# FFN, weight product and scores as 64x64 array tiles, two pairs of sums in turn

## The chip, the cores and the metric

The kernel runs on one core of a Trainium2 chip. The metric is the device time of one execution in microseconds. Where two kernels are compared, the ratio is the mean time of the one's fast runs over the mean of the other's from the same rounds on the same chip, so it is not quite the ratio of the medians quoted beside it. A ratio difference is turned into microseconds with 391 us for the kernel before.

The engines are TensorE (PE; its weight loads are PEld), VectorE (DVE), ScalarE (ACT), GpSimd (POOL) and SyncE (SP).

## The reference

Attention with RMS-normalised q and k (8 batches, 12 heads, 448 tokens, 64 per head), whose output, 3584 tokens by 768, goes through an FFN whose two up-projections are multiplied:

```python
q_n, k_n = rmsnorm(q, g_q), rmsnorm(k, g_k)
attn = softmax(q_n @ k_n.T / 8)
x = (attn @ v)                       # to (3584, 768)
out = (((x @ w1) * (x @ w2)) @ w3) @ w_out
```

The kernel computes `w3 @ w_out` once (the "weight product", w34) and works in bfloat16 with float32 sums.

## The kernel before

The program is a loop of 87 steps, called slots here. In each but the last three, TensorE computes two blocks of scores, ACT their exponentials; then comes (in most slots) a "v set", the product of probabilities with v or with ones; then fillers: FFN sums that keep TensorE busy; and last the "preps" of later heads: squares and alphas on ACT, reductions and scalings on DVE. Of PSUM the sums take eight banks: two score tiles of two banks each, and four banks for all other sums.

```python
sc_psum = ctx.enter_context(tc.tile_pool(name="sc_ps", bufs=2, space=PSUM))
mm_psum = ctx.enter_context(tc.tile_pool(name="mm_ps", bufs=4, space=PSUM))
# ...
def narrow(ps, n, lhsT, rhs, start, stop):          # one 128x128 block as four 128x32 tiles
    for h in range(4):
        nc.tensor.matmul(out=ps[32*h : 32*h+32, 0:n], lhsT=lhsT[:, 32*h : 32*h+32], rhs=rhs,
                         start=start, stop=stop, tile_position=(0, 32*h))

def ffn1_a(b, fi):                                   # x @ w1; ffn1_b (w2) likewise, evicted by DVE
    ps = mm_psum.tile([128, 512], FP, tag="mm", name="pa")
    for c in range(CM):
        narrow(ps, S, w1s[:, c, fi*128 : (fi+1)*128], xT[b][:, c, :], c == 0, c == CM - 1)
    a_sb = ffn_pool.tile([128, S], BF, tag="a_sb", name="a_sb")
    nc.scalar.copy(out=a_sb, in_=ps[:, 0:S])         # the ACT copy of the argument below
    # ...
# ...
for t in range(max(todo) + 1):
    # ... two qk_exp(n): scores on PE, exponential on ACT
    for i, kind in todo.get(t, []):
        pv_set(i, kind)
    # ... loads
    if t in W34_SLOTS: ...                           # weight product, slots 1 to 13
    elif not w34q:
        fill(int(old * room(t) / every + 0.5))       # so many fillers
    for n, part in mine: ...                         # preps
```

The softmax here doesn't subtract the row's maximum and nothing guards it: scores larger than these inputs give would overflow.

## Time and profile before

| | before |
|---|---|
| time, median of 2 runs | 390.64 us (388.81 to 392.47) |
| PE busy | 372.9 us, 96% |
| ACT busy | 265.5 us, 68% |
| DVE busy | 242.6 us, 62% |
| mean granted TensorE clock | 0.989 |

The last column of a group line is the idle time of its engine just before it and who ended it; for PE it is close to nothing. The prediction shows the lines. One more, from the list of waits (engine, line, whom it waited for, total us, times, longest us):

```profile
PE sc L297 <- ACT P L309: 1.3, 2, 0.8
```

PE practically never stands waiting for ACT to empty a score tile.

### The profile page before, as it was taken

To read this page: it belongs to the slowest core of one execution; us is meant where nothing else is said; L and a number is where in the kernel's file an instruction comes from. 1 tells how busy PE (TensorE), PEld (TensorE's weight loads), DVE (VectorE), ACT (ScalarE), POOL (GpSimd) and SP (SyncE) were. 2 spreads that over 40 slices of the span, in tenths; PEclk is the share of its full clock that TensorE was granted. 3 is DMA by queue.
4 is the path that set the end of the run, shared out by engine and by line. 5 is a ranking of instruction groups with operands and counts; after the bars stand their busy time and mean duration, and the time that the engine had idled before them with its cause. 6 is when DMAs were issued, how large, how long until landed. Compare 5 with 4: busy or idle time off the path is not lost.

```text
span 389.5 us, 17790 instructions
## 1 busy us (share of the span) xinstructions
PE 372.9 (96%) x8053; PEld 193.2 (50%) x8054; DVE 242.6 (62%) x398; ACT 265.5 (68%) x443; POOL 75.6 (19%) x131
## 2 busy tenths in 40 slices
PE   6979999999999997999989999999999999999995
PEld 2435555444544454454544554445544554556563
DVE  4789864557758774776568676667676685234232
ACT  3579896778688873888678956797788856730210
POOL 2525446322022202202202202201221000000000
PEclk9889999999999999999999999999999999999999
DMA  7999999769778939849969969958989565004005
GB/s 182 225 235 233 239 229 153 120 101 164 158 171 157 175 79 217 185 67 156 183 158 146 148 132 208 176 123 140 211 164 148 66 159 91 3 3 125 2 22 145
DMA packets 92975, 56.47 MB, mean 145 GB/s; under 512 B 56932, under 2 KB 86884, under 8 KB 92900
## 3 DMA queue, kind: packets, MB, share of 16 engines
q1 hardware_dynamic: 70208, 42.35, 51.7%
q0 software_dynamic: 21952, 12.33, 23.7%
q8 instruction: 63, 1.03, 1.1%
q10 hardware_dynamic: 740, 0.66, 0.7%
q14 instruction: 12, 0.10, 0.1%
HBM read 46.66 MB, written 11.01 MB: 148 GB/s over the span
## 4 chain that ended last, share of the span: by engine, by line
PE 78%; DMA 9%; DVE 4%; ACT 4%; SPq 3%; issue 2%; DVEq 0%; ACTq 0%
PE pa L354 17%; PE pb L354 17%; PE po L354 14%; PE pv L322 13%; PE sc L297 9%; PE wps L354 5%; DMA out_dram<-o_sb 5%; DMA k_sb<-in_k_dram 2%; SPq L129 2%; PE qkT_ps L272 2%; DVE ssq L214 2%; ACT P L309 1%; DVE o_sb L430 1%; DMA q_sb<-in_q_dram 1%; PE w3T_ps L367 1%
## 5 line engine op out<-in xcount | busy, mean ns | idle before, releaser
L309 ACT ACTIVATE P<-sc 128x896 bf16<-128x896 f32 x144 | 125.1, 913 | 29.4 <-PE sc L297 29.4
L354 PE MATMUL pa<-xT,w1s 128*32 128x448 bf16 x1536 | 83.9, 353 | 0.7 <-DVE xT L337 0.7
L354 PE MATMUL pb<-xT,w2s 128*32 128x448 bf16 x1536 | 83.8, 352 | 0.0
L152 POOL DMA_DIRECT2D v_sb<-in_v_dram x72 | 43.8, 620 | 200.5 <-PE pv L322 174.5
L354 PE MATMUL po<-w34s,abT 128*32 128x384 bf16 x1792 | 77.5, 326 | 2.8 <-DVE o_sb L430 2.8
L410 DVE TENSOR_TENSOR abT<-pb,a_sb 128x448 bf16<-128x448 f32 x64 | 39.9, 623 | 60.4 <-PE pb L354 46.5
L214 DVE TENSOR_REDUCE ssq<-sq 128x16 f32<-128x1024 f32 (+1 forms) x50 | 58.2, 1169 | 11.6 <-ACT sq L203 11.6
L397 ACT CAST a_sb<-pa 128x448 bf16<-128x448 f32 x64 | 33.9, 530 | 43.5 <-PE pa L354 43.5
L354 PEld LDWEIGHTS <-abT 128*32 128x32 bf16 x1792 | 48.1, 97 | 29.6 <-issue 3.3
L354 PEld LDWEIGHTS <-w1s 128*32 128x32 bf16 x1536 | 40.4, 97 | 34.3 <-issue 4.9
L354 PEld LDWEIGHTS <-w2s 128*32 128x32 bf16 x1536 | 41.4, 97 | 31.3
L430 DVE COPY o_sb<-po 128x384 f32<-128x384 f32 x56 | 30.5, 556 | 41.0 <-DMA out_dram<-o_sb 21.4
L297 PE MATMUL sc<-qkT 64*32 64x448 bf16 x1344 | 48.9, 357 | 1.8 <-ACT P L309 1.3
L236 DVE TENSOR_TENSOR qtmp<-q_sb,alpha 128x512 bf16<-128x512 f32 x48 | 32.9, 685 | 12.7 <-ACT alpha L225 12.4
L322 PE MATMUL pv<-P,v_sb 128*32 128x448 bf16 x576 | 36.0, 356 | 0.0
L337 DVE TENSOR_TENSOR xT<-pv,r 128x448 bf16<-128x448 f32 x48 | 29.6, 617 | 5.6 <-PE pv L322 3.7
L249 DVE TENSOR_TENSOR qks<-k_sb,alpha 128x512 bf16<-128x512 f32 x48 | 32.9, 685 | 0.0
L203 ACT ACTIVATE sq<-q_sb 128x512 f32<-128x512 f32 x48 | 30.2, 630 | 0.0
L203 ACT ACTIVATE sq<-k_sb 128x512 f32<-128x512 f32 x48 | 29.9, 622 | 0.0
L322 PEld LDWEIGHTS <-v_sb 128*32 128x32 bf16 x768 | 16.2, 95 | 24.2 <-issue 15.7
L297 PEld LDWEIGHTS <-qkT 64*32 64x32 bf16 x1344 | 12.3, 89 | 30.1 <-issue 28.8
L309 ACT ACTIVATE Pr<-sc 128x896 bf16<-128x896 f32 x24 | 22.0, 915 | 4.6 <-PE sc L297 4.6
(46 smaller groups left out, 247.2 us busy)
## 6 DMA issues: line engine op xcount, KB each, us to landing
out_dram<-o_sb SPq DMA_DIRECT2D x54, 192.0 KB, 3.5
q_sb<-in_q_dram SPq DMA_DIRECT2D x23, 256.0 KB, 3.9
k_sb<-in_k_dram SPq DMA_DIRECT2D x23, 256.0 KB, 4.9
q_sb<-in_q_dram SPq DMA_DIRECT2D x23, 192.0 KB, 4.4
k_sb<-in_k_dram SPq DMA_DIRECT2D x23, 192.0 KB, 5.2
v_sb<-in_v_dram POOLq DMA_DIRECT2D x24, 96.0 KB, 4.2
w3s<-in_moe_w_dram POOLq DMA_DIRECT2D x8, 256.0 KB, 9.7
w_outs<-in_moe_w_out_dram POOLq DMA_DIRECT2D x4, 384.0 KB, 11.9
```

Of the source, the lines that this page charges most:

```text
L152: nc.gpsimd.dma_start(out=dst.rearrange("p h j d -> p h (j d)"), in_=part.rearrange("p h j d -> p h (j d)"),)
L203: nc.scalar.activation(out=sq[:, t], in_=src[:, hs], func=AF.Square)
L214: nc.vector.tensor_reduce(out=s["ssq"][:, slice(*t), hs, :], in_=sq[:, slice(*t)], axis=AX, op=ADD)
L236: nc.vector.tensor_tensor(out=qtmp.transpose([0, 2, 1, 3]), in0=s["q"][:, hs], in1=alpha[:, 0, hs].unsqueeze(3).broadcast_to([NP, 2, J, D] ...
L249: nc.vector.tensor_tensor(out=qks[:, 1].transpose([0, 2, 1, 3]), in0=s["k"][:, hs], in1=alpha[:, 1, hs].unsqueeze(3).broadcast_to([NP, 2, ...
L297: nc.tensor.matmul(out=sc[c0 : c0 + 32, u, 0:S], lhsT=qkT[u * D : (u + 1) * D, pr, 1, k0 : k0 + 32], rhs=qkT[u * D : (u + 1) * D, pr, 0, 0:S],
L309: nc.scalar.activation(out=dst, in_=sc[:, :, 0:S], func=AF.Exp)
L322: nc.tensor.matmul(out=ps[h * HALF : (h + 1) * HALF, :], lhsT=w, rhs=s["P"][:, h, j, :] if j < NF else s["Pr"][:, h % 2, :], start=(j == 0 ...
L354: nc.tensor.matmul(out=ps[32 * h : 32 * h + 32, 0:n], lhsT=lhsT[:, 32 * h : 32 * h + 32], rhs=rhs, start=start, stop=stop, tile_position=( ...
L397: nc.scalar.copy(out=a_sb, in_=ps[:, 0:S])
L410: nc.vector.tensor_tensor(out=abT[bp][:, fi, odd * S : (odd + 1) * S], in0=ps[:, 0:S], in1=a_tiles.pop((b, fi)), op=MULT,)
L430: nc.vector.tensor_copy(out=o_sb[:, nh * NH : (nh + 1) * NH], in_=ps[:, 0:NH])
```

## The change

The intent: scores, FFN and weight product share one tile shape, 64x64, so that TensorE need not change shape between them. A 64x64 tile covers half the depth of a sum, and the two row halves of the array may not write one bank at the same time (point 3 of what the prediction takes from the Trainium skill). So two sums are worked on at once: in turn 0 the upper half adds to sum 0 and the lower to sum 1; in turn 1 they change over. Before it does, the matmuls of turn 0 must be through, which a nop on POOL's sequencer passes on. To hide that wait two pairs go in turn, so that a filler is now four sums in four banks. The weight product is moved into slots 8 to 11.

```diff
-    W34_SLOTS = {1: 2, 2: 1, 3: 2, 4: 3, 5: 1, 6: 1, 7: 3, 8: 1, 9: 1, 10: 2, ...}
+    W34_SLOTS = {1: 2, 2: 1, 3: 1, 4: 1, 5: 1, ...}
-        for c0 in range(0, NP, 32):
+        for c0 in range(0, NP, SC_W):               # SC_W = 64
-    def narrow(ps, n, lhsT, rhs, start, stop): ...
+    def swapped(pairs, n):
+        banks = [[mm_psum.tile([128, 512], FP, tag="mm", name="sw") for _ in range(2)] for _ in pairs]
+        turned = {}
+        for turn in range(2):
+            for p, pair in enumerate(pairs):
+                nk = pair[0][2]
+                for c in range(nk):
+                    for r in range(2):
+                        z = r ^ turn
+                        lhsT, rhs, _ = pair[z]
+                        for h in range(2):
+                            mm = nc.tensor.matmul(
+                                out=banks[p][z][64*h : 64*h+64, 0:n],
+                                lhsT=lhsT(c)[64*r : 64*r+64, 64*h : 64*h+64],
+                                rhs=rhs(c)[64*r : 64*r+64],
+                                start=(turn == 0 and c == 0), stop=(turn == 1 and c == nk - 1),
+                                tile_position=(64*r, 64*h), ...)
+                            if turn == 1 and (c, r, h) == (0, 0, 0):
+                                after(mm, turned[p])
+                if turn == 0:
+                    turned[p] = nc.gpsimd.nop()
+                    after(turned[p], mm)
+                if turn == 1:
+                    yield p, banks[p]
+    # w34_unit, ffn1, ffn2: two pairs each, evictions as before
-        for fi in range(CF):
-            fillers.append(ffn1_a); fillers.append(ffn1_b)        # shortened
+        for fi in range(0, CF, 2):
+            fillers.append(lambda b=b, fi=fi: ffn1(b, fi))
     # ... (the rest of the diff follows from this)
```

More of the change, by code (lines that the diff above doesn't have):

```diff
@@ L71 @@
     LAG = 8
+    SC_W = 64
     UNITS = 3.0
@@ L82 @@
     PREP = {'load': -7, 'sq0': -5, 'red0': -5, 'sq1': -4, 'red1': -4, 'alpha': -3, 'sc0': -3, 't0': -1, 'sc1': -2, 't1': -1}
-    W34_SLOTS = {1: 2, 2: 1, 3: 2, 4: 3, 5: 1, 6: 1, 7: 3, 8: 1, 9: 1, 10: 2, 11: 2, 12: 3, 13: 2}
+    W34_SLOTS = {1: 2, 2: 1, 3: 1, 4: 1, 5: 1, 6: 1, 7: 1, 8: 1, 9: 1, 10: 1, 11: 1, 12: 1, 13: 1}
     w1s = const.tile([128, CM, DFF], BF, name="w1s")
@@ L297, in qk_exp @@
                 nc.tensor.matmul(
-                    out=sc[c0 : c0 + 32, u, 0:S],
-                    lhsT=qkT[u * D : (u + 1) * D, pr, 1, k0 : k0 + 32],
+                    out=sc[c0 : c0 + SC_W, u, 0:S],
+                    lhsT=qkT[u * D : (u + 1) * D, pr, 1, k0 : k0 + SC_W],
                     rhs=qkT[u * D : (u + 1) * D, pr, 0, 0:S],
@@ L350, in w34_evac, with after @@
             nc.vector.tensor_copy(out=dst, in_=src)
-    def narrow(ps, n, lhsT, rhs, start, stop):
-        for h in range(4):
-            nc.tensor.matmul(
-                out=ps[32 * h : 32 * h + 32, 0:n],
-                lhsT=lhsT[:, 32 * h : 32 * h + 32],
-                rhs=rhs,
-                start=start,
-                stop=stop,
-                tile_position=(0, 32 * h),
-            )
+    def after(later, earlier):
+        tc.add_manual_dep(
+            later.ins,
+            earlier.ins.name,
+            mybir.DependencyInfo(
+                mybir.DependencyClass.Sync, mybir.DependencyReason.DATA
+            ),
+            reason="the other row half of the array takes over the bank",
+        )
+    def swapped(pairs, n):
+        banks = [
+            [mm_psum.tile([128, 512], FP, tag="mm", name="sw") for _ in range(2)]
+            for _ in pairs
+        ]
+        turned = {}
[8 more added lines that the diff above has]
+                            mm = nc.tensor.matmul(
+                                out=banks[p][z][64 * h : 64 * h + 64, 0:n],
+                                lhsT=lhsT(c)[64 * r : 64 * r + 64, 64 * h : 64 * h + 64],
+                                rhs=rhs(c)[64 * r : 64 * r + 64],
+                                start=(turn == 0 and c == 0),
+                                stop=(turn == 1 and c == nk - 1),
+                                tile_position=(64 * r, 64 * h),
+                                skip_group_check=True,
+                            )
+                            if turn == 1 and (c, r, h) == (0, 0, 0):
[5 more added lines that the diff above has]
+                    yield p, banks[p]
     def w3_transpose(fc):
@@ L370, in w3_transpose, with w34_unit, ffn1 @@
         w34_evac(w3T[:, :, fc * 128 : (fc + 1) * 128], ps, 0)
-    def w34_unit(fc, nh):
-        assert ("o", nh) in issued
-        ps = mm_psum.tile([128, 512], FP, tag="mm", name="wps")
-        for gc in range(CF):
-            lhsT = w3T[:, gc, fc * 128 : (fc + 1) * 128]
-            rhs = w_outs[:, gc, nh * NH : (nh + 1) * NH]
-            if W34_NARROW:
-                narrow(ps, NH, lhsT, rhs, gc == 0, gc == CF - 1)
-            else:
-                nc.tensor.matmul(
-                    out=ps[:, 0:NH], lhsT=lhsT, rhs=rhs,
-                    start=(gc == 0), stop=(gc == CF - 1),
-                )
-        w34_evac(w34s[:, fc, nh * NH : (nh + 1) * NH], ps[:, 0:NH], 1)
-    a_tiles = {}
-    def ffn1_a(b, fi):
-        ps = mm_psum.tile([128, 512], FP, tag="mm", name="pa")
-        for c in range(CM):
-            narrow(
-                ps, S, w1s[:, c, fi * 128 : (fi + 1) * 128], xT[b][:, c, :],
-                c == 0, c == CM - 1,
-            )
-        a_sb = ffn_pool.tile([128, S], BF, tag="a_sb", name="a_sb")
-        nc.scalar.copy(out=a_sb, in_=ps[:, 0:S])
-        a_tiles[b, fi] = a_sb
-    def ffn1_b(b, fi):
+    def w34_unit(fc):
+        pairs = [
+            [
+                (
+                    lambda gc, f=f: w3T[:, gc, f * 128 : (f + 1) * 128],
+                    lambda gc, nh=nh: w_outs[:, gc, nh * NH : (nh + 1) * NH],
+                    CF,
+                )
+                for nh in range(2)
+            ]
+            for f in (fc, fc + 1)
+        ]
+        for p, ps in swapped(pairs, NH):
+            for nh in range(2):
+                w34_evac(
+                    w34s[:, fc + p, nh * NH : (nh + 1) * NH], ps[nh][:, 0:NH], 1
+                )
+    def ffn1(b, f0):
         bp, odd = divmod(b, 2)
@@ L403, in ffn1_b @@
             abT[bp] = big_pool.tile([128, CF, TOK2], BF, tag="big", name="abT")
-        ps = mm_psum.tile([128, 512], FP, tag="mm", name="pb")
-        for c in range(CM):
-            narrow(
-                ps, S, w2s[:, c, fi * 128 : (fi + 1) * 128], xT[b][:, c, :],
-                c == 0, c == CM - 1,
-            )
-        nc.vector.tensor_tensor(
-            out=abT[bp][:, fi, odd * S : (odd + 1) * S],
-            in0=ps[:, 0:S],
-            in1=a_tiles.pop((b, fi)),
-            op=MULT,
-        )
@@ L417 @@
-    o_tiles = {}
-    def ffn2(bp, t, nh):
-        if nh == 0:
-            o_tiles[bp, t] = out_pool.tile([128, DM], FP, tag="o_sb", name="o_sb")
-        o_sb = o_tiles[bp, t]
-        ps = mm_psum.tile([128, 512], FP, tag="mm", name="po")
-        for fi in range(CF):
-            narrow(
-                ps, NH, abT[bp][:, fi, t * 128 : (t + 1) * 128],
-                w34s[:, fi, nh * NH : (nh + 1) * NH], fi == 0, fi == CF - 1,
-            )
-        last = (bp, t) == (B // 2 - 1, 6)
-        nc.vector.tensor_copy(out=o_sb[:, nh * NH : (nh + 1) * NH], in_=ps[:, 0:NH])
-        if nh == 0 and not last:
-            return
-        n0, n1 = (nh * NH, (nh + 1) * NH) if last else (0, DM)
-        for z, c0 in enumerate(range(t * 128, (t + 1) * 128, REST)):
-            bb, f = divmod(c0, S)
-            j, p = divmod(f, NP)
-            _, _, nj, t0, t1 = halves[p // REST]
-            r0 = (2 * bp + bb) * S
-            (nc.scalar if last and z else nc.sync).dma_start(
-                out=out[r0 + t0 : r0 + t1].rearrange("(p j) n -> j p n", j=nj)[
-                    j, :, n0:n1
-                ],
-                in_=o_sb[z * REST : (z + 1) * REST, n0:n1],
-            )
+        pairs = [
+            [
+                (
+                    lambda c, w=w, f=f: w[:, c, f * 128 : (f + 1) * 128],
+                    lambda c: xT[b][:, c, :],
+                    CM,
+                )
+                for w in (w1s, w2s)
+            ]
+            for f in (f0, f0 + 1)
+        ]
@@ new lines, in ffn1, with ffn2 @@
+        for p, ps in swapped(pairs, S):
+            a_sb = ffn_pool.tile([128, S], BF, tag="a_sb", name="a_sb")
+            nc.scalar.copy(out=a_sb, in_=ps[0][:, 0:S])
+            nc.vector.tensor_tensor(
+                out=abT[bp][:, f0 + p, odd * S : (odd + 1) * S],
+                in0=ps[1][:, 0:S],
+                in1=a_sb,
+                op=MULT,
+            )
+    def ffn2(todo):
+        pairs = [
+            [
+                (
+                    lambda fi, bp=bp, t=t: abT[bp][:, fi, t * 128 : (t + 1) * 128],
+                    lambda fi, nh=nh: w34s[:, fi, nh * NH : (nh + 1) * NH],
+                    CF,
+                )
+                for nh in range(2)
+            ]
+            for bp, t in todo
+        ]
+        for p, ps in swapped(pairs, NH):
+            bp, t = todo[p]
+            last = (bp, t) == (B // 2 - 1, 6)
+            o_sb = out_pool.tile([128, DM], FP, tag="o_sb", name="o_sb")
+            for nh in range(2):
+                nc.vector.tensor_copy(
+                    out=o_sb[:, nh * NH : (nh + 1) * NH], in_=ps[nh][:, 0:NH]
+                )
+                if nh == 0 and not last:
+                    continue
+                n0, n1 = (nh * NH, (nh + 1) * NH) if last else (0, DM)
+                for z, c0 in enumerate(range(t * 128, (t + 1) * 128, REST)):
+                    bb, f = divmod(c0, S)
+                    j, pp = divmod(f, NP)
+                    _, _, nj, t0, t1 = halves[pp // REST]
+                    r0 = (2 * bp + bb) * S
+                    (nc.scalar if last and z else nc.sync).dma_start(
+                        out=out[r0 + t0 : r0 + t1].rearrange("(p j) n -> j p n", j=nj)[
+                            j, :, n0:n1
+                        ],
+                        in_=o_sb[z * REST : (z + 1) * REST, n0:n1],
+                    )
@@ L447 @@
     fillers = []
+    rest = []
     def push_ffn(b):
         assert not wq
-        for fi in range(CF):
-            fillers.append(lambda b=b, fi=fi: ffn1_a(b, fi))
-            fillers.append(lambda b=b, fi=fi: ffn1_b(b, fi))
+        for fi in range(0, CF, 2):
+            fillers.append(lambda b=b, fi=fi: ffn1(b, fi))
         bp, odd = divmod(b, 2)
-        for t in range(3, 7) if odd else range(3):
-            for nh in range(2):
-                fillers.append(lambda bp=bp, t=t, nh=nh: ffn2(bp, t, nh))
+        rest.extend((bp, t) for t in (range(3, 7) if odd else range(3)))
+        while len(rest) > 1 or rest and b == B - 1:
+            two, rest[:] = rest[:2], rest[2:]
+            fillers.append(lambda two=two: ffn2(two))
@@ L527 @@
         w34q = [lambda: w3_transpose(0), lambda: w3_transpose(1)]
-        for fc in range(CF + LAG):
-            if fc < CF:
-                w34q.append(lambda fc=fc: w34_unit(fc, 0))
-            if fc + 2 < CF:
-                w34q.append(lambda fc=fc: w3_transpose(fc + 2))
-            if fc >= LAG:
-                w34q.append(lambda fc=fc: w34_unit(fc - LAG, 1))
+        for fc in range(2, CF):
+            w34q.append(lambda fc=fc: w3_transpose(fc))
+        for fc in range(0, CF, 2):
+            w34q.append(lambda fc=fc: w34_unit(fc))
         def prep_part(n, part):
```

## The prediction

> **What bounds the kernel now.** I read the page's busy shares first, then the chain of work that ended last, then the groups of instructions, then the timeline of one loop step ("slot": two score blocks with their two exponentials, one probability-times-v set, then FFN work as filler), and last the POOL timeline of the early stage.
>
> ```profile
> PE 372.9 (96%) x8053; PEld 193.2 (50%) x8054; DVE 242.6 (62%) x398; ACT 265.5 (68%) x443; POOL 75.6 (19%) x131
> ...
> PE 78%; DMA 9%; DVE 4%; ACT 4%; SPq 3%; issue 2%; DVEq 0%; ACTq 0%
> ...
> L309 ACT ACTIVATE P<-sc 128x896 bf16<-128x896 f32 x144 | 125.1, 913 | 29.4 <-PE sc L297 29.4
> L354 PE MATMUL pa<-xT,w1s 128*32 128x448 bf16 x1536 | 83.9, 353 | 0.7 <-DVE xT L337 0.7
> ...
> L354 PE MATMUL po<-w34s,abT 128*32 128x384 bf16 x1792 | 77.5, 326 | 2.8 <-DVE o_sb L430 2.8
> ...
> L397 ACT CAST a_sb<-pa 128x448 bf16<-128x448 f32 x64 | 33.9, 530 | 43.5 <-PE pa L354 43.5
> ```
>
> PE is 96% busy, carries 78% of the chain, and lost only 2.8 us to a late eviction (last column of the po row). ACT waits for PE (29.4 and 43.5 us), PE hardly ever for ACT. One slot in detail:
>
> ```profile
> 238.20 0.57 PE L297 MATMUL sc<-qkT 64*32 64x448 bf16 x16
> 238.70 0.75 PE L322 MATMUL pv<-P,ones 128*32 128x448 bf16 x12
> 239.28 0.36 PE L322 MATMUL pv<-Pr,ones 128*32 128x448 bf16 x4
> 239.47 1.31 PE L354 MATMUL pa<-xT,w1s 128*32 128x448 bf16 x24
> 240.60 1.31 PE L354 MATMUL pb<-xT,w2s 128*32 128x448 bf16 x24
> 241.84 0.57 PE L297 MATMUL sc<-qkT 64*32 64x448 bf16 x16
> ```
>
> Taken start to start: scores 0.50 us, v set 0.77, the FFN sums 1.13 and 1.24, together 3.64. Twenty-four 128x32 matmuls (six full 128x128 blocks) in 1.13 us are about 189 ns a block of 448 columns. What is not streaming is the change of tile shape: 0.11 us from FFN to scores (1.24 - 1.13), 0.13 from scores to v (0.50 - 2 x 0.187).
>
> ```profile
> 57.77 0.62 POOL L152 DMA_DIRECT2D v_sb<-in_v_dram  x1 [1.05 <-DVE qtmp L236]
> 58.89 0.59 POOL L152 DMA_DIRECT2D v_sb<-in_v_dram  x1 [0.50 <-DMA w2s<-in_moe_w_dram]
> 60.36 0.62 POOL L152 DMA_DIRECT2D v_sb<-in_v_dram  x1 [0.88 <-DMA w1s<-in_moe_w_dram]
> 61.76 0.60 POOL L156 DMA_DIRECT2D v_sb<-in_v_dram  x1 [0.78 <-DMA w2s<-in_moe_w_dram]
> ```
>
> These four are the last of POOL's initial loads. Each waits for an earlier transfer, so POOL's queue is clear of weights only at about 62 us; now nobody cares, because POOL has nothing else to do.
>
> **What the Trainium skill says.** (1) "TensorE: Matmul & The Clock Gate", section on why the gap is 56 ns: a warm matmul starts N / 2.4 GHz + about 2.5 ns after the last. For 448 columns that is 189.2 ns; the trace's 189 agrees. So the 128x32 form is already at the array's rate, and no other tiling of the full array has fewer columns to stream. (2) "TensorEngine Tiling (Array Packing)", Key Properties: a change of tiling mode drains TensorE. The 0.11 and 0.13 us agree. (3) The same page, Gotcha 1: different row tiles may not write one PSUM bank at once, and software must see to it. This is why the change needs two banks per pair and a wait at the changeover; no run yet shows it. (4) "PSUM — Partial Sum Buffer", Engine vs sequencer instructions: a nop is executed by the sequencer, which waits only for earlier instructions to be dispatched. Whether the changeover nop on POOL can therefore pass DMAs that still wait in POOL's queue, this trace cannot say.
>
> **The change, part by part.**
>
> *Streaming: 0 us.* A 128x128 block is four 64x64 matmuls instead of four 128x32 ones; FFN and weight product keep their counts, scores halve theirs (1344 to 672), but eight 64x32 tiles ran at once and now four 64x64 do: 448 columns either way.
>
> *Tile-shape changes: about -2.5 us.* FFN and scores now share a shape, but the v set between them stays 128x32. A slot with a v set still changes twice; only the 11 slots without one (from the tenth on) lose both changes: 11 x 0.24 = 2.6.
>
> *Granularity: the main cost.* A filler was one sum of 1.13 to 1.30 us, two or three a slot. It is now two pairs: 4 x 1.13 = 4.5 us (FFN1) or 4 x 1.30 = 5.2 (FFN2). The built instruction order shows that of slots 15 to 82, 38 get one unit and 30 get none. PE's mean work per slot is unchanged, but ACT works in program order, and PE's lead over it is two score buffers. Call a slot with a unit F, an empty one E, and let zero be the end of F's unit. In F, ACT does its two exponentials early, then must wait for the a_sb copies; the second comes only now: start 0.1, end 0.65 (530 ns). Then follow F's squares and alphas, which stand behind the copies: P us. Only then come E's exponentials, 0.913 each, done by 2.5 + P. PE meanwhile does E's scores and v set (0.50 + 0.86 with the change) and then stands before the next slot's second score block until 2.55 + P; with 0.19 + 0.1 + 0.86 after it, the next unit starts at 3.7 + P. If PE set the pace it would start at 2 x 1.36 = 2.7. Each F-E pair thus loses 1.0 + P. There are 19 FFN1 pairs of this kind; from the order, P is 1.25 (two squares) in six, 1.8 in three, 0.56 in two, 0 in eight: 14.0. Sum 19 x 1.0 + 14 = 33 us. For the 10 FFN2 units followed by an empty slot ACT has no copy to wait for, is idle at zero and finishes E's exponentials at 2.1: 0.65 us each, 6.5 in all. One double empty slot adds 1.
>
> *Banks: about +13.* A unit takes all four banks of the pool, where before a bank came round again after three other sums and sets (some 3.5 us). Now a v set's bank is wanted again 1.13 us after the set, by the unit's second pair, while VectorE needs 0.62 for it and may have a 1.2 us reduction ahead. Going through two stretches of the order by hand gave 0 to 0.6 us; I take 0.3 for 38 units and a little more where units follow each other.
>
> *Early stage: about +13.* The weight product (512 matmuls, 20 us) moves from slots 2 to 13 into slots 8 to 11, two halves at once. Slots 1 to 7 become ACT-bound (scores, squares) and end only about 3 us earlier; slots 8 to 11 cost 6.6 us each; slots 12 to 14 are empty and again at ACT's pace of about 3. Without more waits, slot 15 starts some 5 us later than the 73.9 of before. In addition the first changeover wants its nop at about 45, and POOL has all weight loads and a v load ahead of it in program order: 62 if it must be through with them, about 53 if the sequencer runs some DMAs ahead. I take a stall that makes the total +13 here (range 5 to 20).
>
> *Tail: +2.* The last units have nothing to overlap but each other; eviction of a pair by ACT then DVE (0.53 + 0.62) is just longer than the 1.13 of the other pair, and the final pair evicts two halves in a row.
>
> Sum: -2.5 + 33 + 6.5 + 1 + 13 + 13 + 2 = +66, so 456. The waits overlap in part (a late bank gives ACT time to catch up), so I take 450.
>
> **Rivals.** (a) The changeover is free and ACT's lag is absorbed: then only the shape changes remain and the time is about 388. For it: ACT is busy only 68%. Against it: ACT's order puts copies ahead of squares and exponentials, and two score buffers cannot bridge a 4.5 us unit. (b) Row halves with weights of 64 columns stream worse than quarters, or each changeover drains: 96 pairs of changeovers at 0.1 to 0.2 us would add 10 to 20 more, 465. Against it: the scores already use row halves at full rate. (c) POOL's nop is the main cost, at v loads in every stage: four descriptors of 0.62 us stand before a unit's nop in many slots. Against it: POOL reaches them a whole slot earlier. If wrong, 470 and more. (d) The early stage dominates and the steady one costs little: about 410.
>
> **Range and chances.** The steady loss could be half of what I sum (420), or banks and the nop could add 30 (480). Nothing supports a gain over 2%: the shape changes saved are 2.5 us of 390. Faster 0.03, within 2% 0.06, slower 0.91.
>
> **What would show it.** FFN groups of 24 matmuls still about 1.13 us (if longer, the streaming step is wrong). PE's wait for ACT before scores, 1.3 us now, should grow to some 30 to 50 us, and the granted clock stay high. PE's waits before FFN matmuls on DVE or ACT should show some 10 us, and one wait on POOL near 45 us of 5 to 17. Slot pairs should take about 9 us where two slots took 7.3. If slot pairs stay near 7.3, my account of ACT's order is wrong.

## The result, and the profile after

The changed kernel takes 472.01 us (median of 2 runs, 471.28 to 472.75) against 390.64. The ratio is 1.2075 (95% interval 1.193 to 1.222): slower by about 81 us, inside the stated range but above the stated 450.

From the page of the changed kernel: busy shares, granted clock in 40 slices, and the chain's shares.

```profile
PE 393.9 (84%) x7382; PEld 237.7 (50%) x7382; DVE 244.3 (52%) x398; ACT 265.5 (56%) x443; POOL 75.5 (16%) x131
...
PEclk9869679999998999999998999899999999999998
...
PE 53%; ACT 16%; DMA 12%; DVE 12%; issue 4%; POOL 1%; SPq 0%; DVEq 0%; ACTq 0%; POOLq 0%
...
L298 PE MATMUL sc<-qkT 64*64 64x448 bf16 x672 | 59.5, 366 | 30.8 <-ACT P L310 26.2
```

PE is now 84% busy, its share of the chain fell from 78 to 53%, and ACT (4 to 16%) and DVE (4 to 12%) took most of what it lost, although their own busy time has hardly changed. Work was not added; engines wait for each other. (PE's busy time did rise, from 372.9 to 393.9 us: a matmul before a wait is drawn longer than its turn, as told below, and more of them ran at half the clock.) The chain in order of time (start, length, what) shows one turn of it:

```profile
241.38 4.57 PE sw L379 x96
245.95 0.02 issue
245.97 0.53 ACT a_sb L440
246.51 0.23 ACT lnv L225
...
246.89 1.13 ACT sq L204 x2
248.03 1.62 ACT P L310 x2
249.65 0.04 issue
249.69 0.59 PE sc L298 x4
250.28 1.62 PE pv L323 x16
251.89 1.17 PE sw L379 x8
```

A unit ends at 245.95; only then does ACT copy the second sum, then alphas and squares, then two exponentials, and only at 249.69 may PE do the next slot's second score block. From unit to unit it is 251.89 - 241.38 = 10.5 us, the longest of the 19 FFN1 pairs of this kind in the trace; on average they take 9.5. The unit itself is not slow: 96 matmuls in 4.57 us are 1.14 per 24, as before. The waits of PE in the same trace:

```profile
PE sc L298 <- ACT P L310: 26.2, 45, 1.7
PE sw L379 <- POOLq L391: 14.5, 1, 14.5
PE sw L379 <- DVE xT L338: 9.6, 11, 1.3
PE sw L379 <- ACT r L333: 5.6, 6, 1.5
PE sc L298 <- ACT Pr L310: 3.0, 7, 0.4
```

The first and the last are waits for exponentials (29.2 us), the third and fourth for a v set's bank (15.2), the second the changeover nop. In the trace each v set that PE waits for on DVE stands directly behind a reduction or a scaling of the preps, and those on ACT behind two exponentials. The early stage, TensorE and below it POOL:

```profile
44.78 2.14 PE L379 MATMUL sw<-w_outs,w3T 64*64 64x384 bf16 x46 [0.90 <-DMA w_outs<-in_moe_w_out_dram]
61.44 4.58 PE L379 MATMUL sw<-w_outs,w3T 64*64 64x384 bf16 x64 [14.52 <-POOLq L391]
```

```profile
59.69 1.31 POOL L153 DMA_DIRECT2D v_sb<-in_v_dram  x2 [0.66 <-DMA w2s<-in_moe_w_dram]
61.39 0.60 POOL L157 DMA_DIRECT2D v_sb<-in_v_dram  x1 [0.38 <-DMA w2s<-in_moe_w_dram]
```

Turn 1 starts at 61.44, just after POOL's last queued load (61.39) has got past its own wait. The nop did not overtake DMAs that were still waiting.

Split by three marks, the first FFN matmul, the start of the last batch's FFN and the end of the span:

| stretch | before | after | difference |
|---|---|---|---|
| start to first FFN matmul | 71.5 | 96.0 | +24.5 |
| first FFN matmul to the last batch's FFN | 356.2 - 71.5 = 284.7 | 435.5 - 96.0 = 339.5 | +54.8 |
| rest | 33.3 | 35.5 | +2.2 |

An idle time in the profile starts at the modelled end of the last matmul. A block of four score matmuls that takes about 0.19 us start to start is drawn 0.38 long, so each wait contains about 0.19 us more than its idle figure. With that the steady stretch (the middle row) is nearly accounted for, as an estimate. Of the waits above, it holds 28.1 us for exponentials (49 times) and 14.5 for banks (16 times). So: exponentials 28.1 + 49 x 0.19 = 37, banks 14.5 + 16 x 0.19 = 18, one late transfer of q and k 1.7, three spells of 3.4 us at half the clock (from 147.0, 249.4 and 297.2 us) up to 5; less 6 for the six waits of the same stretch before, and less 2.5 for changes of shape saved (the prediction's figure, not measured). Together 53 of 54.8.

### The profile page after: what moved, and what is told of

Its sections match the earlier page's. It is cut to its first block, busy times and chain, and to the rows that moved or that the text cites. A ratio compares the mean times of both kernels' runs of the same rounds, so it can differ in the third digit from the quotient of the medians.

```text
span 471.0 us, 16496 instructions
## 1 busy us (share of the span) xinstructions
PE 393.9 (84%) x7382; PEld 237.7 (50%) x7382; DVE 244.3 (52%) x398; ACT 265.5 (56%) x443; POOL 75.5 (16%) x131
## 4 chain that ended last, share of the span: by engine, by line
PE 53%; ACT 16%; DMA 12%; DVE 12%; issue 4%; POOL 1%; SPq 0%; DVEq 0%; ACTq 0%; POOLq 0%
PE sw L379 47%; ACT P L310 8%; DMA w3s<-in_moe_w_dram 5%; DVE ssq L215 3%; PE pv L323 3%; ACT sq L204 3%; ACT a_sb L440 3%; DMA w2s<-in_moe_w_dram 2%; DMA v_sb<-in_v_dram 2%; DVE qtmp L237 2%; PE sc L298 2%; DVE xT L338 2%; DVE qks L250 2%; DMA qkT<-qks 1%; DVE o_sb L465 1%
## 5 line engine op out<-in xcount | busy, mean ns | idle before, releaser
L379 PE MATMUL sw<-xT,w2s 64*64 64x448 bf16 x1536 | 153.3, 354 | 9.9 <-ACT r L333 4.9
L379 PE MATMUL sw<-xT,w1s 64*64 64x448 bf16 x1536 | 159.9, 355 | 0.0
L379 PEld LDWEIGHTS <-w1s 64*64 64x64 bf16 x1536 | 91.5, 108 | 35.1 <-issue 11.9
L441 DVE TENSOR_TENSOR abT<-sw,a_sb 128x448 bf16<-128x448 f32 x64 | 40.0, 625 | 122.2 <-ACT a_sb L440 122.2
L379 PEld LDWEIGHTS <-w2s 64*64 64x64 bf16 x1536 | 87.6, 108 | 29.6 <-issue 17.1
L440 ACT CAST a_sb<-sw 128x448 bf16<-128x448 f32 x64 | 34.0, 532 | 106.2 <-PE sw L379 106.2
L298 PE MATMUL sc<-qkT 64*64 64x448 bf16 x672 | 59.5, 366 | 30.8 <-ACT P L310 26.2
L379 PE MATMUL sw<-w34s,abT 64*64 64x384 bf16 x1792 | 77.8, 323 | 5.2 <-DVE xT L338 5.0
L379 PEld LDWEIGHTS <-abT 64*64 64x64 bf16 x1792 | 57.9, 107 | 24.4 <-issue 10.7
L465 DVE COPY o_sb<-sw 128x384 f32<-128x384 f32 x56 | 28.6, 553 | 40.8 <-PE sw L379 40.8
L379 PE MATMUL sw<-w_outs,w3T 64*64 64x384 bf16 x512 | 24.2, 341 | 16.1 <-POOLq L391 14.5
```

What stands on the lines that cost most here:

```text
L298: nc.tensor.matmul(out=sc[c0 : c0 + SC_W, u, 0:S], lhsT=qkT[u * D : (u + 1) * D, pr, 1, k0 : k0 + SC_W], rhs=qkT[u * D : (u + 1) * D, pr, ...
L379: mm = nc.tensor.matmul(out=banks[p][z][64 * h : 64 * h + 64, 0:n], lhsT=lhsT(c)[64 * r : 64 * r + 64, 64 * h : 64 * h + 64], rhs=rhs(c)[6 ...
L440: nc.scalar.copy(out=a_sb, in_=ps[0][:, 0:S])
L441: nc.vector.tensor_tensor(out=abT[bp][:, f0 + p, odd * S : (odd + 1) * S], in0=ps[1][:, 0:S], in1=a_sb, op=MULT,)
```

## The experiments

The outputs are right. No run shows whether TensorE could wait for its own turn 0 without another engine.

| run | median us | ratio to before | 95% interval |
|---|---|---|---|
| the changed kernel | 472.0 | 1.2075 | 1.193 to 1.222 |
| e1_nop_on_sync | 499.1 | 1.2742 | 1.266 to 1.283 |
| e2_coarse_quarters | 409.7 | 1.0466 | 1.041 to 1.052 |
| e3_product_back | 447.0 | 1.1416 | 1.135 to 1.148 |
| e4_scores_64 | 390.0 | 0.9958 | 0.991 to 1.001 |
| e5_squares_before_copies | 419.7 | 1.0668 | 1.060 to 1.074 |
| e6_quarters_same_banks | 437.1 | 1.1122 | 1.107 to 1.118 |
| e8_one_pair | 423.3 | 1.0772 | 1.072 to 1.082 |
| e9_set_between | 410.6 | 1.0443 | 1.039 to 1.050 |
| e10_nop_split | 458.5 | 1.1751 | 1.171 to 1.180 |
| e11_before_sc64_preps_first | 388.1 | 0.9949 | 0.991 to 0.998 |
| e12_between_preps_first | 402.9 | 1.0350 | 1.029 to 1.041 |
| e13_both_repairs | 426.0 | 1.0929 | 1.088 to 1.098 |

**The nop on another sequencer.** On the changed kernel:

```diff
-                    turned[p] = nc.gpsimd.nop()
+                    turned[p] = nc.sync.nop()
```

> The changed kernel with one edit: the changeover nop goes to SyncE's sequencer instead of POOL's. Theory (the 14.5 us wait of PE near 45 us is POOL's queue of weight loads): that wait goes and the time falls by 12 to 17 us, to about 457. Rival (the nop stands behind PE's own matmuls, or the weights bind anyway): no change, 472. A third way: SyncE's queue holds loads and stores that wait too, and new PE waits on SyncE of over 5 us in all take the gain back.

The third way came true. The first FFN matmul starts at 80.7 instead of 96.0, so the early wait was POOL's queue. But SyncE's queue, with its loads and stores, made new waits all along the steady part (34.5 of the 37.9 us below after 94 us), and the whole became slower:

```profile
PEld L379 <- SPq L391: 37.9, 19, 3.5
PE sw L379 <- SPq L391: 30.5, 16, 3.1
```

**The same granularity with the old tiles.** On the kernel before: four sums to a filler, one after the other, each in its own bank.

```diff
-            fillers.append(lambda b=b, fi=fi: ffn1_a(b, fi))
-            fillers.append(lambda b=b, fi=fi: ffn1_b(b, fi))
+            fillers.append(lambda b=b, fi=fi: [(ffn1_a(b, f), ffn1_b(b, f)) for f in (fi, fi + 1)])
     # ... (four sums of ffn2 likewise)
```

> The kernel before, with its 128x32 tiles, its one-by-one banks and its early stage, but with fillers of four sums in one piece, as many and in the same slots as in the changed kernel. Theory (the steady loss is granularity against ACT's program order): 415 to 425. By the pair's reckoning the second copy now ends 0.5 us before the filler does, so an FFN1 pair loses the larger of 0.65 and about P - 0.1 (19 us in all), FFN2 pairs 6.5, a double empty slot 1, together 26, plus a few us of lower clock. Rival 1 (granularity is harmless, row halves and banks cost it all): below 398. Rival 2 (granularity is all of the steady loss): 445 to 450.

409.7, below the expected span: the pure size of the filler costs 0.0466 x 391 = 18 us. Its waits for exponentials are 14.5 us in 34 pieces, with 0.19 for each about 21:

```profile
PE sc L297 <- ACT P L309: 12.0, 28, 0.5
PE sc L297 <- ACT Pr L309: 2.5, 6, 0.4
```

There is no wait for a v set's bank. So neither rival holds: granularity is harmful, but it is a third of the steady loss, less than the theory had.

**The weight product as it was.** On the changed kernel: `w34_unit`, its order and W34_SLOTS from the kernel before.

> The changed kernel with the weight product put back as it was (128x32 tiles, one sum at a time, slots 1 to 13). Theory: the early stage loses its 20 us, so 450 to 454, and slot 15 starts near 74 us instead of 94. Rival (the early delay was hidden slack, ACT would have been waited for later anyway): 460 or more.

447, a little better than expected: 1.2075 - 1.1416 = 0.066, or 26 us, for the early stage. Its first FFN matmul starts at 71.5, 24.5 earlier; slot 15 starts at 69.6, not near 74, as slot 14 has no FFN sums here. None of the early loss was hidden slack. Its waits, with which the next versions are compared, are nearly those of the changed kernel without the early one:

```profile
PE sc L298 <- ACT P L310: 26.4, 45, 1.7
PE sw L390 <- DVE xT L338: 9.6, 11, 1.3
PE sw L390 <- ACT r L333: 4.9, 5, 1.5
PE sc L298 <- ACT Pr L310: 2.5, 6, 0.4
```

**Scores alone.** On the kernel before: score tiles 64 wide instead of 32.

> The kernel before with the scores alone in 64x64 tiles. Theory (streaming does not depend on the tile shape, a change of shape costs the same): 390, within 0.7%. Rival (64-column weights load or start more slowly): 168 score blocks at 0.05 us or more each, 399 and above.

0.9958, its interval just reaching 1: as expected, half the instructions and the same time.

**Preps ahead of the filler.** On e3, from slot 15 on:

```diff
+            for n, part in mine:
+                if part[0] != "t" and part not in ("load", "v"):
+                    prep_part(n, part)
             if t in W34_SLOTS: ...
             elif not w34q:
                 fill(...)
-            for n, part in mine: ...        # was here (shortened)
```

> The kernel with the product back (447 us), with the squares, alphas, reductions and scalings of a slot issued ahead of its filler, so that they stand before the copies in ACT's order. Theory (P sits between the late copy and the exponentials): PE's wait for the exponentials, 29 us there, falls by about 14 and the time to 430 to 436. Rival (the copy alone or VectorE sets the pace): under 4 us of change; or slower, if reductions and scalings that now stand before the products on VectorE hold up banks.

419.7: this order alone gives back 0.0748 x 391 = 29 us, twice what was expected, and the lines say why. PE's waits in this run:

```profile
PE sc L298 <- ACT P L310: 16.0, 46, 1.1
...
PE sc L298 <- ACT Pr L310: 2.6, 6, 0.4
```

Waits for exponentials fell from 28.9 us (26.4 and 2.5 in e3) to 18.6. The bank waits (9.6 and 4.9 in e3) are gone from the list altogether: DVE's reductions and scalings no longer stand between the unit's products and the eviction of the next v set, nor ACT's squares before its exponentials and evictions. With four banks held, the bank term was thus a matter of the order on DVE and ACT; but e2, with the old order and banks taken one by one, has none either, so it needs both. Exponentials 10.3, banks 14.5 and 16 waits fewer at 0.19 are 28 of the 29 us.

**Old tiles, the same banks and ends.** On e3, inside the unit:

```diff
-                for c in range(nk):
-                    for r in range(2): ...              # 64x64, row halves changing over
+                for c in range(turn * nk // 2, (turn + 1) * nk // 2):
+                    for z in range(2):
+                        lhsT, rhs, _ = pair[z]
+                        narrow(banks[p][z], n, lhsT(c), rhs(c), c == 0, c == nk - 1)
```

> The kernel with the product back, units of two pairs and four banks taken and finished at the same points, but each matmul a 128x32 quarter over the full depth: the two sums of a pair take half their depth in turn 0 and half in turn 1, so no row half and no changeover wait. Theory (row halves stream at full rate and the hidden changeover is free; what costs is that both sums end together and the banks): 443 to 451, as with row halves, PE's bank waits again about 14 us. Rival (row halves or the changeover themselves cost): about 410, as the coarse quarters with one sum after the other.

437.1, below the expected span, between the two and much nearer to row halves. Going from e2 to e6 (same tiles, but sums that end together and four banks held) costs 0.0656, 26 us; going from e6 to e3 (row halves and the changeover) 0.0294, 11 us. Its waits:

```profile
PE sc L298 <- ACT P L310: 21.6, 37, 1.4
PE sw L355 <- DVE xT L338: 9.0, 11, 1.3
PE sw L355 <- ACT r L333: 3.9, 3, 1.3
PE sc L298 <- ACT Pr L310: 2.5, 6, 0.4
```

The bank waits are back without any row half. Of the 11 us, exponentials and banks explain 28.9 - 24.1 = 4.8 and 14.5 - 12.9 = 1.6, and some ten fewer waits at 0.19 another 2; here the first sum of a pair ends one block earlier than the second, so its copy starts earlier. The traces of the two show two more differences in the steady part: e3 waits once for a late transfer of q and k (1.3 us), and it has one spell of 3.4 us at half the clock there (up to 1.7 lost), e6 none. That is about all of it, so nothing is left that would point to slower streaming in row halves.

**One pair to a filler.** On e3: units of one pair, two banks, nothing between its turns.

> The kernel with the product back, but with one pair to a filler (2 banks, 2.3 us) and so each changeover exposed: its second turn waits for its own first turn's last matmul and the nop. Theory (granularity and banks cost most of it, the changeover would cost little over its latency): bank waits near zero, about 0.3 to 0.5 us of PE idle at each of 92 changeovers, so 392 + 28 to 46 = 420 to 438. Rival (changeovers are cheap, 0.1 us): near 402. Rival (they are worse than the granularity): 450 or more.

423.3, as the theory expected. Waits for exponentials and v-set banks are not among its waits of PE; instead weight loads stand at every changeover:

```profile
PEld L390 <- POOLq L402: 49.1, 92, 0.8
```

Around one of them matmuls start at 231.94 and 232.42, 0.48 us apart where the rhythm is 0.19. That is 0.29 lost, times 92 about 27 us; the ratio says 30.

**The v set between the turns.** On e8: turn 0, v set, turn 1; in slots without a v set the scores stand between.

> As with one pair to a filler, but the v set (or, in slots without one, the scores) is issued between the two turns, so it hides the changeover; the last units go two pairs in turn. 64x64 row halves throughout FFN and scores. Theory (nothing is wrong with the row halves, only with when their sums end and what they hold): 390 to 402; some 15 second pairs of a slot keep an exposed changeover or a late bank. Rival (row halves cost by themselves): 420 or more.

410.6, missed: the changeover is hidden (its waits for POOL's nop are 5.1 us in 17 pieces instead of 49.1 in 92), which gained 13 us, but 17 remain against the kernel before. PE's list has 6.9 us for v-set banks, 4.5 for two late evictions before v sets and 3.8 for exponentials.

**The same, preps first.** e9 with the edit of e5.

> The v set between the two turns, and preps ahead of the filler. Without the second edit it stands 18 us above before. Theory (both sums still end together at the end of a slot, with the squares behind the copies): the order gives back a third to a half, 400 to 404. Rival (the 18 us are late banks of v sets between turns, which this does not touch): 408 to 412.

402.9, in time as expected; but by the ratios only 3.6 us came back, less than the expected third to a half of 18 and less than the medians suggest, because the kernel before was also quicker in that round. About 14 us remain. No group of waits before its matmuls is over 4 us; weight loads wait 6.2 us for the products on DVE and 5.6 for nops. I did not find one cause: it stays open.

**The nop split.** The changed kernel, SyncE's nop for the weight product only.

> The changed kernel with the changeover nop of the weight product alone on SyncE, that of the FFN on POOL as it was. Theory (of the early 20 us the wait behind POOL's weight loads is 15, the concentration into four slots 5; POOL costs nothing later): PE's 14.5 us wait gone, no SyncE waits after the early stage, the first FFN matmul near 81 us instead of 96, and 455 to 459. Rival (the time comes back later as other waits): 465 or more.

458.5 and 1.1751. The first FFN matmul comes at 81.9, 14.1 earlier than in the changed kernel, the 14.5 us wait is gone and no wait on SyncE or POOL is left. The rest of the list is nearly what it was (26.2, 9.6, 5.2, 3.0), so POOL's nop costs nothing here once its queue is clear. By this mark the early stage thus divides into 14 us of nop and 24.5 - 14.1 = 10 us of concentration.

**Both repairs.** e10 with the edit of e5.

> The changed kernel with both repairs: the weight product's nop on SyncE and the preps ahead of the filler. Theory (the two losses are independent): 472 - 15 - 27 = 430, 427 to 434. Rival (they overlap): 440 or more.

426.0, just under the expected span. From the ratios, 1.2075 - 0.0324 - 0.0748 would be 1.1003; it is 1.0929, 3 us less, which is within the intervals. The losses are independent as far as these runs can tell, and 36 us stay.

**A better version of the kernel before.** Scores 64 wide and preps first, on the kernel before.

> The kernel before with scores in 64x64 tiles and the squares, alphas, reductions and scalings ahead of the filler. PE waits only 1.3 us for exponentials there, so theory: 387 to 391, within 1% of before. Rival (the order has slack to give here too): 384 or less. Rival (products wait behind reductions on VectorE and hold banks): 394 or more.

388.1 and 0.9949, its interval below 1: faster than both kernels, though against the kernel before by half a per cent only. As e4 alone gave 0.9958, nothing shows that the order of the preps adds to it.

## Why the prediction was right

The direction and the range were right, and the mechanism is the one it named. By the ratios of e2, e6 and e3 the 81 us divide into 18 for the size of the filler, 26 for sums that end together in four banks held, 11 for row halves with their changeover, and 26 for the early stage. The early stage was sized too small, the sum was then discounted where nothing overlapped, and a loss of clock was left out. That the steady terms add up to 51 against 54.8 measured is partly luck: exponentials came out some 3 us below their term, banks some 5 above, and the clock's up to 5 us and the 6 us of waits that the kernel before had there were in no term.

- *Streaming costs nothing:* held. A unit runs at 1.14 us per 24 matmuls, and e4 and the balance of e6 and e3 agree.
- *The shape changes saved are small:* e4 and the steady sum fit it, but no run measured the 2.5 us by itself.
- *ACT's program order, 33 + 6.5 + 1 = 40.5 us:* held. The waits come to about 37 with their hidden part. The trace has the 19 FFN1 pairs that were counted. From a unit's end to the next unit's start they take 4.1 us on average (2.6 to 6.1), where 3.7 + P was reckoned, 4.4 on average, and 2.7 without a wait: some 27 us lost instead of 33. The FFN2 pairs lose the 0.65 each that was reckoned. Pairs take 9.5 us on average, banks included, where "about 9" was the sign named. In the pair shown above P is 1.5, not 1.8, and half the clock lengthens what follows, so that its 10.5 against the reckoned 4.57 + 3.7 + 1.8 = 10.1 proves less than it seems. e5, which takes P away, left 18.6 us of idle in 52 waits, about 28 with the hidden part, against 26.5 reckoned for the pairs without P.
- *Banks, 13:* about 18. The reason given, a reduction ahead of the eviction on DVE, is what the trace shows for two thirds of it and e5 removes; the other third is evictions on ACT behind exponentials.
- *Early stage, 13 (5 to 20):* this step failed in size. By the prediction's own mark, the start of slot 15, it is 94.0 - 73.9 = 20.1; e10 starts slot 15 at 79.9. So the concentration cost 6.0, where 5 was reckoned, and the nop 14.1, where 8 was: the 13 fits a nop at 53, that is a sequencer which runs ahead of its DMAs. It was 61.4, close to the 62 also named. By the first FFN matmul the loss is 24.5, because slot 14 had FFN sums before and has none now, and the time followed this mark (25 us between the changed kernel and e3). One reading was off: of the four POOL loads shown, said to wait for an earlier transfer each, the first is put down to a DVE instruction.
- *Tail, 2:* 2.2.
- *"The waits overlap in part, so I take 450":* this step failed. The undiscounted sum was 456, and with 24.5 for the early stage it would have been 467.
- *"The granted clock stay high":* failed in part. The mean fell from 0.989 to 0.96. The trace has half the clock from 20.7 to 30.9 us, where TensorE waits for preps and for the loads of w3, from 51.5 to 65.2, in the early stall and just after it, and in the three spells of the steady stretch. One of these follows the waits at 247 to 250 us: the next twelve v-set matmuls are drawn 1.31 us long instead of 0.75. From 94 to 435.5 the mean is still 0.99, so this was a few us and no more.

Of the rivals, (a) fell with the result; (b) was at most 11 us with the changeover, all but explained by ends, banks, a late transfer and the clock; (c) was right for the early stage and wrong for the rest (e10), so that its "470 and more" is near to 472 by chance; (d) fell, as the steady part is two thirds of the loss.

## What to carry to other kernels

When TensorE is full, a filler's size, the moment its sums end and what stands behind them in the other engines' program order are a cost of their own, even if no work is added; put work that others wait for ahead of copies that must wait for a long unit. A signal sent through another engine waited here for the transfers queued there before it (14.5 us on POOL, 30.5 in all on SyncE), so look at what is queued at that time, not at how busy the engine is. And two score buffers did not bridge a unit of 4.6 us.

## What the Trainium skill lacked or had wrong

- "PSUM — Partial Sum Buffer", Engine vs sequencer instructions, says that a nop waits only for the dispatch of earlier instructions. It doesn't say that software DMAs which wait for a semaphore count as not yet dispatched: here the nop's effect came at 61.44 us, after POOL's last waiting load had started at 61.39.
- "TensorEngine Tiling (Array Packing)", Key Properties and Gotcha 1, gives no price for a change of mode or for ordering two row halves on one bank. Here a change of mode cost 0.11 to 0.13 us, and an exposed changeover through another sequencer about 0.29 us (e8).
- "TensorE: Matmul & The Clock Gate", Part 1, has the cold state after at least one idle window of about 3.4 us, though its section on a second HAM failure mode tells of short idles between groups of matmuls that do it too. Here the clock was at half from 249.4 to 252.8 us, and in the 3.4 us before that TensorE had been idle for only 1.9 (a wait of 1.7 us, a score block, the start of another wait), so a window that is idle in part can be enough.
- The same page, LDWEIGHTS, has the time of a weight load grow with its columns (columns / 1.2 ns, so 27 and 53 ns for 32 and 64). In the traces a load of 32 columns is recorded as 97 ns and one of 64 as 107 to 108 ns.
- No page warns that the drawn length of a matmul hides part of a wait: four score matmuls are drawn 0.38 us long where 0.19 is their pace, so an idle figure before TensorE understates each wait by about 0.19 us.
